# Conversion pieces of the gate weights tied to their place in VectorE's queue

## The chip, the cores and the metric

One Trainium2 chip, one core. The metric is device time in microseconds of one execution of the whole program, weights and inputs in HBM, outputs written to HBM.

## The reference

Three stages in float32, one after the other.

```python
# 1. local attention: 4 batches x 8 heads, 512 tokens + 32 global ones, head size 64
s_ll = where(|i - j| <= 32, q_l @ k_l.T / 8, -1e9);  s_lg = q_l @ k_g.T / 8
out_l = softmax([s_lg, s_ll]) @ [v_g, v_l]
out_g = softmax(q_g @ [k_g, k_l].T / 8) @ [v_g, v_l]
x = [out_g, out_l] as 2304 tokens x 512
# 2. gated layer: 512 -> 1536 -> 512
g = x @ w_gate
x = (silu(g) * (x @ w_val)) @ w_out
# 3. eight experts, 288 tokens each, given out greedily by descending logit
logits = x @ gate;  token -> expert, capacity 288
out[mask_e] = relu(x[mask_e] @ w1[e]) @ w2[e]
```

The weights of stage 2 arrive in 64-bit words, which the kernel itself turns into float32: 512 x 2 words of 32 bits per row and piece.

## The kernel before, in words

**Attention.** A unit is one batch, one half of the tokens and one pair of heads; 32 units, four of them to a half, and each has two windows `w` of 128 queries. A step is one unit and one window, in three parts that run as a pipeline over consecutive steps. `st_a` multiplies queries and keys on TensorE into the single PSUM bank S (L281), and VectorE adds the mask and takes the maximum in one instruction per head (L290), after which ScalarE makes the exponentials (L296). `st_b` transposes them (L313, banks PTa and PTb by turns) and `split_p` makes a high half on ScalarE (L304) and a low half on VectorE (L305). `st_c` multiplies with the values' high and low halves (L326, bank PV), and after the second window VectorE scales the result into `x` (L332, L333, L337). `unit_split` prepares the values: ScalarE scales and rounds (L247, L248), GpSimd takes the low half (L249). A batch's value scale (`v_scale`) needs both of its `gv` loads first; these use the same three buffers as the units. After four units `x0_t` transposes the half and splits it (L354 to L357): this is one block of 256 tokens for stage 2.

**Weights' conversion.** Stage 2's weights come in 12 slices `f` of three pieces each: gate, value and output weights. `words(f, j)` turns a piece's 64-bit words into float32 with three VectorE instructions (L173, L174, L175); each call then issues the next weight load on SyncE's queue (`load_w`, L124; three buffers). For output weights (j = 2) ScalarE makes a high half and VectorE the low one (L179, L180). For gate and value weights ScalarE sums the magnitudes (L182), TensorE adds them over the partitions (`total`, L148, into the bank that the next gate will use), `pow2` makes a power of two of the sum on VectorE (L154, L156, L157), and with it ScalarE and VectorE write the two float16 halves (L198, L199). `conv` is a generator of these pieces: five per slice, three for the first.

**Token blocks.** `first_blocks` takes three blocks of 256 tokens through the 12 slices together, since each slice's weights serve all three. Per slice and block, `gates` runs 24 matmuls (L486) into one of two G banks, ScalarE a tanh (L491), VectorE two products (L493, L495), ScalarE the high half `hh` (L497) and GpSimd the low half `hl` (L499); `out` then runs six matmuls (L509) into the block's two accumulators, one block later. The accumulators of the second and third block are the banks S, PV, PTa and PTb, so their output matmuls start only when the attention of the first four halves is done. The six other blocks follow (`moe_block`), each with the rest of the attention pulled in between; then the routing and the experts.

**Order of the work.** The program is written as generators that are stepped by turns: in the first attention one conversion step in nine attention steps (27 of these to a half, 108 in all), then one conversion step for each of the nine yields per slice of `first_blocks`. This is not the order of the queues. The tile framework schedules instructions by its own simulated clock (L1116): where an engine is free there, it takes the ready instruction that comes first in the program, so that an instruction whose inputs are ready early moves up past those that still wait. Each engine then works through its queue in the fixed order that comes out.

Of the kernel before, what the change touches and what calls it, by code (L numbers as in the profile page):

```python
# [13 lines left out]
OP = mybir.AluOpType  # L14
# [11 lines left out]
WIN = 224  # L26
UW = 1376
UK = 352
P15 = 32768.0
BIG = 3.0e38  # L30
# [3 lines left out]
def body(ctx, tc, units, gk, gv, wts, w2g, w1, w2, cst, cst2, out):  # L34
# [14 lines left out]


# [111 lines left out]
    def conv():  # L162
# [4 lines left out]
        def words(f, j):  # L167
            t = WR.pop((f, j))
            if j == 2:
                x = cv[0].tile([128, 512], I32, name="wx", bufs=2)  # L170
            else:
                x = wp_[:, f + 1, j].rearrange("p h c -> p (h c)").bitcast(I32)
            ve.tensor_scalar(x, t[:, :, 1], 3, 0x3FFFFFFF, op0=OP.logical_shift_left, op1=OP.bitwise_and)  # L173
            ve.scalar_tensor_tensor(x, t[:, :, 1], -0x40000000, x, op0=OP.bitwise_and, op1=OP.bitwise_or)  # L174
            ve.scalar_tensor_tensor(x, t[:, :, 0], 29, x, op0=OP.logical_shift_right, op1=OP.bitwise_or)  # L175
            load_w()
            x = x.bitcast(F32)
            if j == 2:
                sc.activation(oh[:, f, :], x, AF.Copy)  # L179
                ve.tensor_tensor(ol[:, f, :], x, oh[:, f, :], op=OP.subtract)  # L180
            else:
                sc.activation(junk[:, :512], x, AF.Abs, bias=tiny, accum_out=st[f][1][:, j:j + 1])  # L182
            st[f][0].append(x)

        for f in range(NF + 1):
            g = f - 1
            if g >= 0:
                xw, m = st.pop(g)
# [6 lines left out]
            if g >= 0:  # L195
                for j in range(2):
                    h, l = wp_[:, g, j, 0], wp_[:, g, j, 1]
                    sc.activation(h, xw[j], AF.Identity, scale=s[:, j:j + 1])  # L198
                    ve.scalar_tensor_tensor(l, xw[j], s[:, j:j + 1], h, op0=OP.mult, op1=OP.subtract)  # L199
# [73 lines left out]
    def st_a(u, w):  # L273
# [15 lines left out]
        for h in range(2):  # L289
            ve.tensor_tensor_reduce(sm[:, h], S[:, h, :WIN], mask[:, mv], -0.125, BIG, OP.add, OP.min,  # L290
                                    mx[:, h:h + 1])
# [8 lines left out]
    def split_p(pt, n, k):  # L300
# [4 lines left out]
        ve.scalar_tensor_tensor(pl[:q, :c], pt[:q, :c], P15, ph[:q, :c], op0=OP.mult, op1=OP.subtract)  # L305
# [146 lines left out]
    class Moe:  # L452
# [24 lines left out]
        def gates(self, f):  # L477
# [17 lines left out]
            ve.scalar_tensor_tensor(h[:, :n], t[:, :n], ib[:, 1, f:f + 1], pg[:, 1, :n], op0=OP.mult, op1=OP.mult)  # L495
# [21 lines left out]
    def first_blocks():  # L517
# [3 lines left out]
        for f in range(NF):  # L521
            while conv_done[0] < f:
                step_conv()
            for m in ms:
                yield from m.gates(f)
                yield
# [3 lines left out]
                yield  # L530
# [102 lines left out]
    for _ in first_blocks():  # L633
        step_conv()
# [51 lines left out]
    def small(shape, name, dt=F32, bufs=2):  # L686
# [5 lines left out]
    NS, SY = (mybir.DependencyInfo(c, mybir.DependencyReason.DATA)  # L692
              for c in (mybir.DependencyClass.NoSync, mybir.DependencyClass.Sync))
# [426 lines left out]
```

## Time and profile before

| | |
|---|---|
| runs, median of 3 | 987.62 us (985.96 to 990.65) |
| profiled execution: time, span | 987.89 us, 986.1 us |
| mean granted TensorE clock | 0.935 of full speed |
| TensorE busy | 876.8 us, 89% of the span |
| VectorE busy | 604.6 us, 61% |
| ScalarE busy | 473.6 us, 48% |
| GpSimd busy | 336.6 us, 34% |

The profiled execution is one of the program's runs; its span is what the trace covers, and 1.8 us of its time lie around it. Busy shares are averages over stages that differ: the first attention runs to about 160 us, the three token blocks to about 291 us, the other blocks with the rest of the attention to about 650 us, routing and experts to the end.

### The profile page before, as it was taken

The page shows a single profiled execution, that of the slowest core. Times are in us where ns is not written, and L with a number is a line of the kernel's source. Part 1 is how long each engine was busy: PE and PEld are TensorE (multiplying, and loading weights), DVE is VectorE, ACT ScalarE, POOL GpSimd, SP SyncE. Part 2 cuts the span into 40 slices and gives each one's busy share as a digit, 9 for nine tenths or more (in the row PEclk, how much of TensorE's full clock was granted, in tenths as well). Part 3 has the DMA queues.
Part 4 walks back from the last instruction along what each step waited for, and adds up shares of the span by engine and source line. Part 5 has one row for each costly group of instructions (what it writes and reads, how often), then busy time and mean ns, then how long its engine had stood idle before and what let it go on. Part 6 is the DMA issues. An engine that isn't in the chain of part 4 may idle for free.

```text
span 986.1 us, 19528 instructions
## 1 busy us (share of the span) xinstructions
PE 876.8 (89%) x7532; PEld 736.0 (75%) x7532; DVE 604.6 (61%) x1849; ACT 473.6 (48%) x1068; POOL 336.6 (34%) x324
## 2 busy tenths in 40 slices
PE   4766679999999999989989989996399899999996
PEld 3554558887788878768768757784298889889996
DVE  6998998442215749569587466265776667663210
ACT  6657676542225746457464333231344555455541
POOL 1211433431111212212211101121247867777941
PEclk9786889999999999999989999997689999999998
DMA  8766643010011321142321020000534564446610
GB/s 318 252 238 231 213 171 120 2 56 1 2 43 61 107 76 52 58 129 90 133 101 55 27 73 1 1 23 12 192 106 134 173 208 158 156 132 215 192 49 25
DMA packets 28497, 108.10 MB, mean 110 GB/s; under 512 B 3572, under 2 KB 3572, under 8 KB 28276
## 3 DMA queue, kind: packets, MB, share of 16 engines
q1 hardware_dynamic: 25332, 97.94, 29.6%
q0 software_dynamic: 3072, 8.92, 2.5%
q8 instruction: 59, 0.97, 0.4%
q14 instruction: 34, 0.28, 0.1%
HBM read 97.92 MB, written 8.91 MB: 108 GB/s over the span
## 4 chain that ended last, share of the span: by engine, by line
PE 56%; DVE 17%; DMA 13%; issue 7%; ACT 3%; POOL 3%; SPq 1%; another core or an unknown queue 0%; POOLq 0%; ACTq 0%; DVEq 0%
PE G L486 24%; PE X L509 10%; PE A L951 5%; DMA er<-w 4%; DMA wr<-wts 4%; PE A L935 3%; DMA xg<-xs,idx 2%; POOL el L882 2%; DMA unit<-gv 2%; PE rt L768 2%; DVE ptl L305 1%; DVE junk L445 1%; DVE sm L290 1%; DVE wp L175 1%; DVE kk L269 1%
## 5 line engine op out<-in xcount | busy, mean ns | idle before, releaser
L486 PEld LDWEIGHTS <-wp 128*128 128x128 f16 x2592 | 232.7, 100 | 79.2 <-issue 51.6
L486 PE MATMUL G<-xth,wp 128*128 128x256 f16 (+1 forms) x1344 | 237.9, 271 | 4.6 <-ACT xth L356 3.4
L499 POOL TENSOR_TENSOR hl<-th,hh 128x256 fp32r<-128x256 f32 (+1 forms) x108 | 80.4, 745 | 367.3 <-ACT hh L497 260.4
L486 PE MATMUL G<-xtl,wp 128*128 128x256 f16 (+1 forms) x672 | 177.8, 271 | 3.0 <-DVE xtl L357 3.0
L882 POOL TENSOR_TENSOR el<-er,eh 128x1024 fp32r<-128x1024 f32 x60 | 141.7, 2389 | 45.6 <-ACT eh L881 45.3
L493 DVE SCALAR_TENSOR_TENSOR th<-th,G 128x256 f32<-128x256 f32 (+1 forms) x108 | 43.4, 402 | 125.6 <-ACT th L491 125.4
L491 ACT ACTIVATE th<-G,ib 128x256 f32<-128x256 f32 (+1 forms) x108 | 49.5, 459 | 115.4 <-PE G L486 113.0
L881 ACT ACTIVATE eh<-er 128x1024 fp32r<-128x1024 f32 x64 | 66.7, 1056 | 58.0 <-DMA er<-w 51.5
L497 ACT ACTIVATE hh<-th 128x256 fp32r<-128x256 f32 (+1 forms) x108 | 43.5, 404 | 89.6 <-DVE th L495 89.0
L935 PE MATMUL A<-xh,eh 128*128 128x272 f32 x256 | 78.0, 305 | 0.0
L951 PE MATMUL A<-fh,eh 128*128 128x272 f32 x256 | 76.4, 301 | 0.0
L935 PE MATMUL A<-xh,el 128*128 128x272 f32 x256 | 74.9, 294 | 0.0
L935 PE MATMUL A<-xl,eh 128*128 128x272 f32 x256 | 74.9, 293 | 0.0
L951 PE MATMUL A<-fl,eh 128*128 128x272 f32 x256 | 73.8, 289 | 0.4 <-DVE fl L940 0.4
L951 PE MATMUL A<-fh,el 128*128 128x272 f32 x256 | 74.1, 291 | 0.0
L296 ACT ACTIVATE pb<-sm,mx 128x224 f32<-128x224 f32 x128 | 60.3, 472 | 24.7 <-DVE mx L290 17.2
L281 PE MATMUL S<-unit 128*128 128x224 f32 x128 | 43.9, 480 | 21.6 <-DVE mx L290 16.5
L445 DVE SCALAR_TENSOR_TENSOR junk<-xr,w2gt 128x512 f16<-128x512 f32 x80 | 58.8, 735 | 3.8 <-ACT xr L422 3.1
L509 PE MATMUL X<-oh,hh 128*128 128x512 f32 x156 | 58.0, 444 | 1.3 <-ACT hh L497 1.3
L940 DVE SCALAR_TENSOR_TENSOR fl<-A,fh 128x272 fp32r<-128x272 f32 x64 | 27.9, 439 | 50.0 <-ACT fh L939 45.4
L509 PE MATMUL X<-oh,hl 128*128 128x512 f32 x156 | 54.6, 422 | 0.0
L495 DVE SCALAR_TENSOR_TENSOR th<-th,ib,G 128x256 f32<-128x256 f32 (+1 forms) x108 | 49.9, 463 | 2.7
(288 smaller groups left out, 2141.2 us busy)
## 6 DMA issues: line engine op xcount, KB each, us to landing
er<-w SPq DMA_DIRECT2D x64, 512.0 KB, 5.6
unit<-units SPq DMA_DIRECT2D x32, 688.0 KB, 4.1
wr<-wts SPq DMA_DIRECT2D x36, 512.0 KB, 4.8
unit<-gv SPq DMA_DIRECT2D x16, 640.0 KB, 3.9
gkr<-gk SPq DMA_DIRECT2D x8, 608.0 KB, 3.4
xs<-xr SPq DMA_DIRECT2D x17, 256.0 KB, 2.0
w2gt<-w2g SPq DMA_DIRECT2D x1, 2048.0 KB
wp<-cst SPq DMA_DIRECT2D x1, 512.0 KB, 4.8
```

The costliest lines, as they stand in the source:

```text
L281: te.matmul(S[:, h, :WIN], t[:, UK + 256 * h + 128 * w:UK + 256 * h + 128 * w + 128], t[:, kw], start=True, stop=True)
L296: sc.activation(pb[:, h], sm[:, h], AF.Exp, bias=mx[:, h:h + 1], scale=-1.0, accum_out=RS[u][:, w, h:h + 1])
L445: ve.scalar_tensor_tensor(junk[:, :DM], xr, 1.0, w2gt[:, e], op0=OP.mult, op1=OP.mult, accum_out=L[:, c, e:e + 1])
L486: te.matmul(pg[:, j, :n], wp_[:, f, j, a, o], x[:, d, :n], start=(i == 0), stop=(i == 11))
L491: sc.activation(th[:, :n], pg[:, 0, :n], AF.Tanh, scale=ib[:, 0, f:f + 1])
L495: ve.scalar_tensor_tensor(h[:, :n], t[:, :n], ib[:, 1, f:f + 1], pg[:, 1, :n], op0=OP.mult, op1=OP.mult)
L499: gp.tensor_tensor(hl[:, :n], h[:, :n], hh[:, :n], op=OP.subtract)
L509: te.matmul(self.px[t], a[:, 128 * t:128 * t + 128], w[:, f, :], start=(f == 0 and i == 0), stop=(f == NF - 1 and i == 2))
L881: sc.activation(h, r, AF.Copy)
L882: q = (ve if j == 0 and i < 4 else gp).tensor_tensor(l, r, h, op=OP.subtract)
L935: behind(te.matmul(pa_[:, :CAP], a[:, s], x[:, d], start=(i == 0), stop=(i == 11)))
L951: behind(te.matmul(py[:, :CAP], a[:, s], x[:, f], start=(i == 0), stop=(i == 23)))
```

## The change

`mark` remembers the latest of certain VectorE instructions: the masked maximum (L290), the low half of the probabilities (L305) and a gate's second product (L495). `after` adds, to the first instruction of each words piece (L173) and to each gate/value low half (L199), an edge to the one remembered at that point of the program. Both are on VectorE and the edge has no semaphore: it only says that the one stands behind the other in the queue. In `first_blocks` the yields now carry the slice, and a conversion step is taken only while the conversion is less than two slices ahead; before, one was taken at every yield.

```diff
--- before.py
+++ after.py
@@ -47,6 +47,19 @@
     wk = pa.enter_context(tc.tile_pool(name="wk", bufs=2))
     ps = pa.enter_context(tc.tile_pool(name="ps", bufs=1, space=bass.MemoryType.PSUM))
 
+
+    NS, SY = (mybir.DependencyInfo(c, mybir.DependencyReason.DATA)
+              for c in (mybir.DependencyClass.NoSync, mybir.DependencyClass.Sync))
+    TURN = []
+
+    def mark(ins):
+
+        TURN[:] = [ins]
+
+    def after(ins):
+
+        if TURN:
+            tc.add_manual_dep(ins.ins, TURN[0].ins.name, NS, reason="its turn")
 
     UB = 3
     UT = {}
@@ -170,7 +183,7 @@
                 x = cv[0].tile([128, 512], I32, name="wx", bufs=2)
             else:
                 x = wp_[:, f + 1, j].rearrange("p h c -> p (h c)").bitcast(I32)
-            ve.tensor_scalar(x, t[:, :, 1], 3, 0x3FFFFFFF, op0=OP.logical_shift_left, op1=OP.bitwise_and)
+            after(ve.tensor_scalar(x, t[:, :, 1], 3, 0x3FFFFFFF, op0=OP.logical_shift_left, op1=OP.bitwise_and))
             ve.scalar_tensor_tensor(x, t[:, :, 1], -0x40000000, x, op0=OP.bitwise_and, op1=OP.bitwise_or)
             ve.scalar_tensor_tensor(x, t[:, :, 0], 29, x, op0=OP.logical_shift_right, op1=OP.bitwise_or)
             load_w()
@@ -196,7 +209,7 @@
                 for j in range(2):
                     h, l = wp_[:, g, j, 0], wp_[:, g, j, 1]
                     sc.activation(h, xw[j], AF.Identity, scale=s[:, j:j + 1])
-                    ve.scalar_tensor_tensor(l, xw[j], s[:, j:j + 1], h, op0=OP.mult, op1=OP.subtract)
+                    after(ve.scalar_tensor_tensor(l, xw[j], s[:, j:j + 1], h, op0=OP.mult, op1=OP.subtract))
                 yield g
             if f < NF:
                 words(f, 1)
@@ -287,8 +300,8 @@
         sm = wk.tile([128, 2, WIN], F32, name="sm", tag="sm")
         mx = wk.tile([128, 2], F32, name="mx")
         for h in range(2):
-            ve.tensor_tensor_reduce(sm[:, h], S[:, h, :WIN], mask[:, mv], -0.125, BIG, OP.add, OP.min,
-                                    mx[:, h:h + 1])
+            mark(ve.tensor_tensor_reduce(sm[:, h], S[:, h, :WIN], mask[:, mv], -0.125, BIG, OP.add, OP.min,
+                                         mx[:, h:h + 1]))
         if w == 0:
             RS[u] = wk.tile([128, 2, 2], F32, name="rs")
         pb = wk.tile([128, 2, WIN], F32, name="pb")
@@ -302,7 +315,7 @@
         pl = wk.tile([128, 4, 128], F16, name="ptl")
         q, c = n
         sc.activation(ph[:q, :c], pt[:q, :c], AF.Copy, scale=P15)
-        ve.scalar_tensor_tensor(pl[:q, :c], pt[:q, :c], P15, ph[:q, :c], op0=OP.mult, op1=OP.subtract)
+        mark(ve.scalar_tensor_tensor(pl[:q, :c], pt[:q, :c], P15, ph[:q, :c], op0=OP.mult, op1=OP.subtract))
         return ph, pl
 
     def st_b(u, w):
@@ -492,7 +505,8 @@
             t = th
             ve.scalar_tensor_tensor(t[:, :n], th[:, :n], 1.0, pg[:, 0, :n], op0=OP.add, op1=OP.mult)
             h = th
-            ve.scalar_tensor_tensor(h[:, :n], t[:, :n], ib[:, 1, f:f + 1], pg[:, 1, :n], op0=OP.mult, op1=OP.mult)
+            mark(ve.scalar_tensor_tensor(h[:, :n], t[:, :n], ib[:, 1, f:f + 1], pg[:, 1, :n],
+                                         op0=OP.mult, op1=OP.mult))
             hh = wk.tile([128, 256], F32R, name="hh", bufs=3)
             sc.activation(hh[:, :n], h[:, :n], AF.Copy)
             hl = wk.tile([128, 256], F32R, name="hl", bufs=3)
@@ -522,12 +536,13 @@
             while conv_done[0] < f:
                 step_conv()
             for m in ms:
-                yield from m.gates(f)
-                yield
+                for _ in m.gates(f):
+                    yield f
+                yield f
                 if last is not None:
                     last[0].out(last[1])
                 last = m, f
-                yield
+                yield f
         last[0].out(last[1])
 
     def moe_block(k):
@@ -630,8 +645,9 @@
         i += 1
         if i % 9 == 0:
             step_conv()
-    for _ in first_blocks():
-        step_conv()
+    for f in first_blocks():
+        if conv_done[0] < f + 2:
+            step_conv()
     cvs.close()
     w2p = pa.enter_context(tc.tile_pool(name="w2p", bufs=1))
     w2gt = w2p.tile([128, NE, DM], F32, name="w2gt")
@@ -689,8 +705,6 @@
     IDX, EV, ROUTED, GATHERED = {}, {}, [], []
 
     VISIT = []
-    NS, SY = (mybir.DependencyInfo(c, mybir.DependencyReason.DATA)
-              for c in (mybir.DependencyClass.NoSync, mybir.DependencyClass.Sync))
 
     def behind(ins):
 
```

## Rows read from the trace of the kernel before

**Rows 1.** Busy tenths of VectorE in 40 slices of the span (page).

```profile
DVE  6998998442215749569587466265776667663210
```

**Rows 2.** Window table: stretch, length, busy us by engine, clock, DMA share.

```profile
0.00:158.00 158.00, 107.95 (x784) 85.08 (x785) 142.83 (x387) 104.71 (x272) 38.40 (x46) 0.81 0.68 236
18.73:75.19 56.46, 40.16 (x307) 30.65 (x306) 55.53 (x149) 35.89 (x95) 11.96 (x10) 0.79 0.72 246
75.19:107.73 32.54, 22.39 (x135) 16.80 (x133) 27.44 (x78) 22.82 (x58) 8.32 (x12) 0.69 0.61 208
...
212.00:290.00 78.00, 78.00 (x577) 60.93 (x576) 17.52 (x39) 18.40 (x41) 13.79 (x19) 1.00 0.02 8
```

**Rows 3.** Timeline of VectorE, L290 of steps 3, 17, 22, 32.

```profile
18.73 0.38 DVE L290 CUSTOM_DVE_ANT_0 sm<-S,mask 128x224 f32<-128x224 f32 x1
...
75.19 0.37 DVE L290 CUSTOM_DVE_ANT_0 sm<-S,mask 128x224 f32<-128x224 f32 x1
...
107.73 0.38 DVE L290 CUSTOM_DVE_ANT_0 sm<-S,mask 128x224 f32<-128x224 f32 x1
...
157.08 0.36 DVE L290 CUSTOM_DVE_ANT_0 sm<-S,mask 128x224 f32<-128x224 f32 x1
```

**Rows 4.** Conversion by line: ns min/median/max, first and last start us.

```profile
L173 DVE TENSOR_SCALAR wp<-wr x24: 386/415/1378, 11.8 to 136.2; 128x512 int32<-128x512 int32 x24
...
L174 DVE SCALAR_TENSOR_TENSOR wp<-wr,wp x24: 655/680/694, 12.2 to 138.0; 128x512 int32<-128x512 int32 x24
...
L175 DVE SCALAR_TENSOR_TENSOR wp<-wr,wp x24: 650/681/1641, 13.2 to 141.1; 128x512 int32<-128x512 int32 x24
L175 DVE SCALAR_TENSOR_TENSOR wx<-wr,wx x12: 672/678/693, 16.7 to 148.2; 128x512 int32<-128x512 int32 x12
...
L180 DVE TENSOR_TENSOR ol<-wx,oh x12: 676/681/693, 18.1 to 151.5; 128x512 fp32r<-128x512 f32 x12
```

**Rows 5.** Groups by line, 0 to 158 us.

```profile
L281 PE MATMUL S<-unit 128*128 128x224 f32 x128 | 43.9, 480 | 21.6 <-DVE mx L290 16.5 <-DMA unit<-units 4.7
...
L326 PE MATMUL PV<-vh,pth 112*128 112x64 f16 x116 | 17.4, 210 | 9.7 <-DVE x L337 8.4 <-ACT pth L304 1.3
...
L326 PE MATMUL PV<-vh,ptl 112*128 112x64 f16 x116 | 16.0, 212 | 7.3 <-DVE ptl L305 7.3
...
L199 DVE SCALAR_TENSOR_TENSOR wp<-wp,pscw 128x512 f16<-128x512 f32 x9 | 6.6, 741 | 0.0
```

**Rows 6.** Timeline of SyncE's DMA queue, 60 to 110 us.

```profile
83.56 13.74 SPq L124 DMA_DIRECT2D wr<-wts  x6
103.18 0.33 SPq L66 DMA_DIRECT2D unit<-units  x1
```

**Rows 7.** Window table for L486 alone.

```profile
0.00:158.00 158.00, 19.85 (x138) 14.80 (x139) 0.81 0.68 236
```

**Rows 8.** Chain that ended last: start us, us, what.

```profile
214.03 2.31 PE G L486 x21
...
287.04 2.31 PE G L486 x21
```

**Rows 9.** L154 by line, and its engine's idle time before it.

```profile
L154 DVE TENSOR_SCALAR pe<-G x12: 147/159/160, 19.4 to 207.9; 128x2 int32<-128x2 int32 x12
...
  PE G L148: 9.4, 6
```

**Rows 10.** Groups by line, 160 to 298 us.

```profile
L499 POOL TENSOR_TENSOR hl<-th,hh 128x256 fp32r<-128x256 f32 x32 | 23.8, 744 | 92.6 <-ACT hh L497 31.2 <-PE PV L509 24.7 <-PE PTb L509 20.0
...
L495 DVE SCALAR_TENSOR_TENSOR th<-th,ib,G 128x256 f32<-128x256 f32 x32 | 15.3, 480 | 1.0
...
L493 DVE SCALAR_TENSOR_TENSOR th<-th,G 128x256 f32<-128x256 f32 x32 | 13.4, 421 | 68.7 <-ACT th L491 68.6
```

**Rows 11.** Timeline from 20 us, GpSimd and VectorE.

```profile
20.88 3.21 POOL L249 TENSOR_TENSOR vl<-unit,vh 112x512 f16<-112x512 f32 x2
...
21.55 1.53 DVE L175 SCALAR_TENSOR_TENSOR wp<-wr,wp 128x512 int32<-128x512 int32 x1
```

## The prediction

> **What bounds the kernel now.** I read the page's slices first, then a window table by stage, then the DVE groups and what PE waits for, and last the two places to which the work moves. VectorE is full from 20 to 160 us and then nearly empty [rows 1]. Up to 158 us it is busy for 142.8 us; ScalarE is busy for 104.7 us, TensorE for 108.0 us at a mean granted clock of 0.81 [rows 2]. At 212 to 290 us it is the other way round: PE is busy for all 78.0 us, DVE for 17.5 us [rows 2]. So the first attention is bound by DVE and the three token blocks by PE.
>
> The attention has 32 steps (unit, window); each has one pair of masked-score reductions (L290). The third step's is at 18.73 us, the 17th at 75.19, the 22nd at 107.73, the last at 157.08 [rows 3]. That is 14 steps of 4.03 us, then five in 32.5 us, where the second batch's value scale is made, then ten of 4.94 us. In the first stretch DVE is busy 55.5 of 56.5 us and ACT 35.9 us, or 2.56 us a step [rows 2].
>
> Why is DVE full? All 36 pieces of words stand in this stretch: the last third instruction of one starts at 148.2 us, the last split of the output weights at 151.5 us [rows 4]. By the program's order 12 conversion steps belong here, one in nine of 108: slices 0 and 1 and two words of slice 2, which makes 8 words, 2 output splits and 4 gate/value splits. The scheduler has hoisted the rest, because their inputs were ready.
>
> **What the change moves.** No instruction is added, none removed, and no semaphore: the new edges only order VectorE's own queue. One word costs 0.415 + 0.680 + 0.681 = 1.78 us, an output split 0.68, a gate/value split 0.74 [rows 4, 5]. Out of the stretch go 28 words (49.7 us), 10 output splits (6.8) and 5 of the 9 gate/value splits (3.7): **60.2 us of DVE**. This is queue time, and not the gain.
>
> *The gain in the attention.* PE is idle for 16.5 us before score matmuls until DVE's maxima, 8.4 us before the value matmuls until DVE has taken the previous unit's result (L337), and 7.3 us until DVE's low halves (L305): **32.2 us** [rows 5]. The bounds: none returns, if a chain through ACT is as late; or the stage shrinks to ACT's 104.7 us, which is 53 us. A second route gives about the same: halfway between 4.03 us and ACT's 2.56 saves 0.74 us a step, 18 us over 24 steps. In the turn, six weight loads in SP's queue held it from 83.56 us for 13.7 us, and the next unit's load went out at 103.18 [rows 6]; with the loads following the pieces some 13 us of this go. That is 31 us. I take 32.2, the measured waits. A step that waits less for DVE will wait next for ACT's exponentials.
>
> *What moves with it.* Every word issues the next weight load on SP. 28 loads less 3 prefetched ones leave the stretch, so that unit and value loads stand behind fewer of them; in the token blocks three per 12 us meet a DMA that is 2% busy [rows 2]. Their wait is for DVE's release of the buffer, and the load of the routing weights, queued behind the last of them on SP, is needed only after the fourth block: nothing. The pieces' ACT work (abs, high halves) goes too, into a stage where ACT is busy for 18.4 of 78 us [rows 2]: nothing, while that cover lasts.
>
> *Gates that fitted into the old stretch.* 138 gate matmuls, 5.75 gates of 24, ran before 158 us [rows 7]. With slice 1's split now the 11th of the 12 steps and less idle PE, I give four. From 214.03 to 287.04 us 18 gates pass, 4.06 us each, of which 2.6 are gate matmuls (2.31 us for 21 of 24) [rows 8]. So 1.75 x 2.6 = **4.6 us** is lost; bounds 0 (all still fit) and 15 (none does).
>
> *The token blocks.* One slice (three gates) lasts 12.17 us on PE. DVE's conversion needs 3 x 1.78 + 0.68 + 2 x 0.74 + three small ones of 0.16 [rows 4, 5, 9] = 8.0 us per slice, the gates 3 x (0.48 + 0.42) = 2.7 us [rows 10]: 10.7 of 12.17 us. It fits, but the pieces come in the first five of nine steps, so two gates meet nearly all of it. The trace has no slice with all of this. Bounds: 0, and 4 us (the slower rival). I take 0.4 us, near the lower end, as the conversion runs two slices ahead of its use and DVE's need lies below PE's: **4 us** over ten slices.
>
> [...] GpSimd's low halves of the values ran from 20.88 us, two in 3.21 us, and inside them a third word instruction took 1.53 us against its median of 0.68 [rows 4, 11]. In the token blocks GpSimd makes one hl of 0.74 us per gate [rows 10]. [...]
>
> *Sum.* 987.9 (profiled execution; span 986.1 and 1.8 around it) - 32.2 + 4.6 + 4 = 964.3. The median of the runs is 987.6, 0.3 less: **964**. The later stages have no conversion in them and shift as they are.
>
> **The rivals.**
> 1. *The stage falls to ACT's time*: 53 us instead of 32.2, 944. For it: DVE also slows ACT, whose queue is idle a third of the time. Against: each step is a chain over PE, DVE, ACT, PE, ACT, DVE with one bank for scores. Chance 0.15.
> 2. *VectorE becomes the bound of the token blocks through GpSimd*: each of three hl holds it for its 0.74 us, 10.7 + 2.2 = 12.9 us against 12.17; some 0.75 us x 10 slices in place of the 4, so 968; with the in-order waits for the scale's matmul (9.4 us in six [rows 9], 1.6 a slice) 14.5, which makes 23 us and 983. For it: rows 11. Against: an hl takes 0.74 of a gate's 4.06 us, and only what DVE starts inside it is held. Chance 0.11.
> 3. *Another wait takes the place of DVE's*: half of the 32.2 stays, as PE at a clock of 0.7 in the turn [rows 2] and ACT's chain are nearly as late: 980. Chance 0.12.
> 4. *It doesn't do what it says*: only the first instruction of a piece is pinned, to a place no earlier than its mark, and the scheduler fills the gaps as tightly: 988. Against: the pin alone forbids the hoist. Chance 0.05.
> 5. *Slower: the bank of the scale.* The matmul that sums a slice's magnitudes takes the bank of the next gate; that gate starts only when DVE has read the sum. Before, the words were done long ahead. Now the second word stands behind the last gate's L495, then 1.78 us and an ACT pass, and if the third word and its split (2.5 us) go ahead of the read on DVE, PE stands for up to 4 us per slice. At 4 x 10 = 40 us it gives 987.9 - 32.2 + 4.6 + 40 = 1000; from 2.8 us per slice on, the gain is gone. For it: DVE waited for that matmul six times [rows 9]. Against: the scheduler sees the wait and orders PE's queue by it. Chance 0.09.
>
> **How the numbers follow.** The forecast (955 to 974) has 0.48. A measurement of this kernel tells about 0.5%, 5 us, from no change. Faster by more: 0.48 + 0.15 + 0.11 and some 0.07 of rival 3 = 0.81; within: 0.05 of rival 3 and rival 4, 0.10; slower 0.09. The range runs from 940, just under rival 1, to 985, which takes in rivals 2 and 3 and leaves out 5 and most of 4.
>
> **What would show it.** Right: in the window up to the last L290, about 32 us earlier than 157, DVE has slack; some 8 words start there, the others among the L495s; the idle of L281, L326 before DVE shrinks below half of 32 us; slices keep 12.2 to 12.6 us. Wrong: words still crowd the attention (4), DVE slack with unchanged pitch (3), PE idle before L486 behind L148 or L154 (5), third word instructions above 1 us beside POOL (2).

## The result, and the profile after

| | before | after |
|---|---|---|
| runs, median of 4 | 987.21 us | 971.30 us |
| lowest to highest | 985.96 to 990.65 | 969.81 to 974.83 |
| profiled execution: time, span | 987.89, 986.1 us | 974.83, 973.1 us |
| mean granted TensorE clock | 0.935 | 0.954 |

The ratio is 0.9839, with a 95% interval of 0.9802 to 0.9875: 1.6% faster. The forecast was 964, the range 940 to 985; the gain is 15.9 us where 23.6 were forecast. The profiled execution after is the slowest of its four, so its own gain is 13.1 us.

In the changed kernel lines of the helpers stand 13 or 14 lower: the masked maximum is L303 (was L290), the score matmul L294 (L281), the value matmul L339 (L326), the words L186 to L188 (L173 to L175), the sum over partitions L161 (L148), its ACT pass L195 (L182), the gate matmul L499 (L486), a gate's second product L508 (L495), GpSimd's low half L513 (L499), the output matmul L523 (L509).

In the profile's rows PE is TensorE, PEld its weight load, DVE VectorE, ACT ScalarE, POOL GpSimd and SP SyncE.

First the page, three rows of its 40 slices of the kernel after. Of these the DVE row answers to [rows 1].

```profile
PE   5777699999999999989989989995498899999996
DVE  3877968888227578489496484266775677674210
PEclk9979899999999999999979999998599999999998
```

VectorE is no longer full from the second to the seventh slice and nearly empty behind them: its work goes on to the tenth. The last pair of masked maxima now starts at 110.91 us instead of 157.08 [rows 3], 46 us earlier. Eight words start before 112 us, the number that was forecast:

```profile
L187 DVE SCALAR_TENSOR_TENSOR wp<-wr,wp x6: 676/692/1530, 22.6 to 102.5; 128x512 int32<-128x512 int32 x6
L187 DVE SCALAR_TENSOR_TENSOR wx<-wr,wx x2: 679/684/689, 39.9 to 81.3; 128x512 int32<-128x512 int32 x2
```

They are not quite the eight that were meant. The second word of slice 2 is tied to the attention's last low half (L318, 114.03 us) and starts at 114.63 us; in its place stands the first word of slice 3, whose edge names the first gate's second product, and that one is at 77.44 us.

The steps of [rows 3] show where the attention became shorter. The third, 17th, 22nd and last pair of maxima are now at 19.04, 55.27, 75.12 and 110.91 us. The three stretches between them, after:

```profile
19.04:55.27 36.23, 28.10 (x275) 22.59 (x272) 30.57 (x104) 30.60 (x90) 9.85 (x9) 1.00 0.55 183
55.27:75.12 19.85, 14.67 (x108) 12.04 (x106) 12.86 (x49) 15.48 (x41) 2.88 (x7) 0.74 0.42 153
75.12:110.91 35.79, 25.35 (x261) 20.46 (x259) 29.43 (x86) 28.79 (x79) 11.69 (x10) 0.95 0.58 184
```

The first 14 steps lost 20.2 us (2.59 us a step instead of 4.03), the turn to the second batch 12.7, the last ten steps 13.6. In the turn both VectorE's pieces and the weight loads in front of the unit loads became fewer; no run separates the two.

Yet only 13 of these 46 us reach the end of the profiled execution. Where they go is best read from one window table: up to the last maxima, from there to the 36th gate of the three token blocks (its second product starts at 290.08 us before and at 275.39 after), and both together. The columns are those of [rows 2]: length, busy time of PE, PEld, DVE, ACT and POOL with the number of instructions, granted clock, DMA's busy share, GB/s. TensorE's idle time is the length less its busy time. The kernel before:

```profile
0.00:157.50 157.50, 107.45 (x780) 84.61 (x781) 142.38 (x385) 104.21 (x271) 37.90 (x44) 0.80 0.68 235
157.50:290.00 132.50, 132.44 (x1000) 105.25 (x999) 47.74 (x115) 51.34 (x118) 35.23 (x62) 1.00 0.06 23
0.00:290.00 290.00, 239.89 (x1777) 189.86 (x1778) 190.12 (x499) 155.55 (x388) 73.13 (x105) 0.89 0.40 138
```

The kernel after:

```profile
0.00:111.50 111.50, 77.14 (x674) 61.68 (x674) 79.49 (x270) 85.59 (x234) 25.87 (x31) 0.94 0.59 199
111.50:275.30 163.80, 152.75 (x1106) 120.13 (x1105) 114.80 (x230) 69.59 (x156) 53.41 (x74) 0.97 0.31 109
0.00:275.30 275.30, 229.89 (x1777) 181.81 (x1778) 194.29 (x499) 155.18 (x388) 79.28 (x105) 0.96 0.42 146
```

The last row of each holds the same 1777 TensorE instructions, so the two can be set against each other as a ledger. Idle time of TensorE in the attention fell from 50.05 to 34.36 us (−15.7). Behind the attention it rose from 0.06 to 11.05 us (+11.0). The 1777 instructions themselves took 10.0 us less, at a mean granted clock of 0.96 instead of 0.89. Together −15.7 + 11.0 − 10.0 = **−14.7 us**, the 36th gate's gain. The rest of the 46 us was never a gain: token-block matmuls that had run in the old attention left it. Of gate matmuls alone 19.40 us stood before 157.5 us, and 3.38 us before 111.5 us after.

That the 10.0 us are the clock's can be seen by matching TensorE's instructions with the granted clock in the two traces, where it stands at one of two levels, 1.00 and 0.50 of full speed (after, 1.00 from 111.5 to 116.3 us and 0.50 from 116.3 to 123.1). A score matmul takes 353 ns (median) at the upper level and 581 at the lower in both kernels, a gate matmul 272 and 421. Before, TensorE was busy for 48.4 us at the lower level on the way to the 36th gate, after for 19.2 us. At these durations 29 us less at the lower level save a third and more, 10 to 11 us: an estimate that agrees with the measured 10.0.

From there on nothing changes by more than 1.2 us. The last gate matmul starts 379.5 us behind the 36th gate before (669.6, so the other blocks end some 20 us behind the 650 given above) and 380.1 us after (655.4); from it to the end of the span it is 316.5 and 317.6 us.

What TensorE waited for in the attention, by line, after (0 to 111.5 us; answers to [rows 5]):

```profile
L294 PE MATMUL S<-unit 128*128 128x224 f32 x128 | 36.9, 417 | 13.6 <-DVE mx L303 8.2 <-DMA unit<-units 5.3
L339 PE MATMUL PV<-vh,pth 112*128 112x64 f16 x120 | 16.0, 197 | 2.9 <-DVE x L350 1.7 <-ACT pth L317 0.8 <-ACT vh L261 0.3
L339 PE MATMUL PV<-vh,ptl 112*128 112x64 f16 x120 | 14.4, 199 | 5.0 <-DVE ptl L318 4.9
```

The three waits for DVE were 16.5, 8.4 and 7.3 us; now they are 8.2, 1.7 and 4.9: 14.8 of 32.2 us remain. Laid over VectorE's own instructions in the traces, these waits show why. Before, VectorE was at work on a conversion piece for 18.1 of the 32.2 us; after, for 3.6 of the 14.8. What is left is in the main the instruction itself that TensorE waits for: 12.2 us of the 16.5 before score matmuls were the maxima's own time, and 7.1 of the 8.2 still are. VectorE is idle for only 0.3 us in the remaining waits.

The same 128 score matmuls take 417 ns instead of 480 in the mean, the value matmuls 197 to 199 instead of 209 to 212: fewer of them ran at the lower clock (of the 128 score matmuls 25 took over 500 ns, and 58 before).

What TensorE waits for behind the attention was nothing before. After, from 111.5 to 275.3 us (waited for: us in total, times, longest):

```profile
PE G L499 <- DVE th L508: 6.9, 10, 2.0
PE PTb L367 <- DVE x L350: 1.9, 1, 1.9
PE PV L339 <- DVE ptl L318: 0.7, 1, 0.7
PE G L161 <- ACT junk L195: 0.6, 4, 0.2
PE PV L339 <- DVE x L350: 0.4, 1, 0.4
```

Two places. At the **seam**, 111.5 to 128 us, TensorE is idle for 4.4 us at a clock of 0.79 (the lower level from 116.3 to 123.1 us). The last unit's scaling (L350) stands behind five instructions of slice 2's words on DVE; their edges name the last low half, and the scaling is not marked:

```profile
114.03 0.68 DVE L318 SCALAR_TENSOR_TENSOR ptl<-PTa,pth 112x512 f16<-112x512 f32 x1
114.63 0.42 DVE L186 TENSOR_SCALAR wp<-wr 128x512 int32<-128x512 int32 x1
114.97 0.42 DVE L186 TENSOR_SCALAR wx<-wr 128x512 int32<-128x512 int32 x1
...
117.11 0.42 DVE L350 TENSOR_TENSOR x<-PV,rs 128x256 f32<-128x256 f32 x1
```

And the first gate matmuls of the third block take 0.42 us each, against 0.27 us later on. In the **slices**, 128 to 275.3 us, it is idle for 6.6 us, nearly all of it before a gate whose G bank DVE has not yet read (L508). Seven slices, from one second product to the same one seven slices later, on DVE's timeline:

```profile
142.67 0.48 DVE L508 SCALAR_TENSOR_TENSOR th<-th,ib,G 128x256 f32<-128x256 f32 x1
...
235.56 0.48 DVE L508 SCALAR_TENSOR_TENSOR th<-th,ib,G 128x256 f32<-128x256 f32 x1
```

92.89 / 7 = 13.27 us a slice, where [rows 8] gave 12.17. In that stretch TensorE is busy for 88.83 us: 12.69 busy and 0.58 idle a slice. Of the 0.52 us that it is busier, 0.38 are the two matmuls of the sum (L161), which the slices of [rows 8] no longer had. Of the idle time 0.43 us a slice is the wait for a G bank and up to 0.16 the wait for the sum's magnitudes. The second product that holds the bank is not behind a piece: VectorE stands idle before it until the tanh is done. One of the seven slices, the others have the same pair of rows:

```profile
166.05 0.42 DVE L506 SCALAR_TENSOR_TENSOR th<-th,G 128x256 f32<-128x256 f32 x1 [1.44 <-ACT th L504]
166.51 0.48 DVE L508 SCALAR_TENSOR_TENSOR th<-th,ib,G 128x256 f32<-128x256 f32 x1
```

What differs is the order on TensorE. The three gates of a slice, 4.06 us apart in the kernel before, now follow one another after 2.7, 3.1 and 7.5 us, so that one gate needs a bank again before the chain of tanh and two products has emptied it.

### The profile page after: what moved, and what is told of

The parts are those of the page before. It is cut to its first block, busy times and chain, and to the rows that moved or that the text cites. A ratio compares the mean times of both kernels' runs of the same rounds, so it can differ in the third digit from the quotient of the medians.

```text
span 973.1 us, 19541 instructions
## 1 busy us (share of the span) xinstructions
PE 865.8 (89%) x7532; PEld 727.4 (75%) x7532; DVE 608.5 (63%) x1849; ACT 472.9 (49%) x1068; POOL 341.6 (35%) x324
## 5 line engine op out<-in xcount | busy, mean ns | idle before, releaser
L499 PEld LDWEIGHTS <-wp 128*128 128x128 f16 x2592 | 235.1, 100 | 85.1 <-issue 57.1
L499 PE MATMUL G<-xth,wp 128*128 128x256 f16 (+1 forms) x1344 | 235.1, 271 | 11.9 <-DVE th L508 8.4
L513 POOL TENSOR_TENSOR hl<-th,hh 128x256 fp32r<-128x256 f32 (+1 forms) x108 | 82.1, 760 | 365.3 <-ACT hh L511 310.7
L499 PE MATMUL G<-xtl,wp 128*128 128x256 f16 (+1 forms) x672 | 177.8, 270 | 3.0 <-DVE xtl L370 3.0
L954 DVE SCALAR_TENSOR_TENSOR fl<-A,fh 128x272 fp32r<-128x272 f32 x64 | 27.9, 439 | 53.7 <-ACT fh L953 52.9
L523 PE MATMUL X<-oh,hh 128*128 128x512 f32 x156 | 57.7, 442 | 1.3 <-ACT hh L511 1.3
L523 PE MATMUL X<-oh,hl 128*128 128x512 f32 x156 | 54.8, 422 | 0.0
L303 DVE CUSTOM_DVE_ANT_0 sm<-S,mask 128x224 f32<-128x224 f32 x128 | 44.6, 384 | 15.0 <-PE S L294 7.2
L508 DVE SCALAR_TENSOR_TENSOR th<-th,ib,G 128x256 f32<-128x256 f32 (+1 forms) x108 | 50.0, 463 | 2.9
```

The source lines that it names most:

```text
L303: mark(ve.tensor_tensor_reduce(sm[:, h], S[:, h, :WIN], mask[:, mv], -0.125, BIG, OP.add, OP.min, mx[:, h:h + 1]))
L499: te.matmul(pg[:, j, :n], wp_[:, f, j, a, o], x[:, d, :n], start=(i == 0), stop=(i == 11))
L508: mark(ve.scalar_tensor_tensor(h[:, :n], t[:, :n], ib[:, 1, f:f + 1], pg[:, 1, :n], op0=OP.mult, op1=OP.mult))
L513: gp.tensor_tensor(hl[:, :n], h[:, :n], hh[:, :n], op=OP.subtract)
L523: te.matmul(self.px[t], a[:, 128 * t:128 * t + 128], w[:, f, :], start=(f == 0 and i == 0), stop=(f == NF - 1 and i == 2))
```

## The experiments

Each was run against the kernel before on the same chip; kernels of different rounds are compared through their ratios, and most of all through the traces. The table gives, for each profiled execution, the start of the last pair of maxima, TensorE's idle time up to the 36th gate, the mean clock up to there, the 36th gate's second product, the last gate matmul, and the ratio with its 95% interval.

| kernel | last max | idle | clock | 36th gate | last gate MM | median us | ratio |
|---|---|---|---|---|---|---|---|
| before | 157 | 50.1 | 0.89 | 290.1 | 669.6 | | 1 |
| after | 111 | 45.4 | 0.96 | 275.4 | 655.4 | 971.3 | 0.9839 [0.9802, 0.9875] |
| nopins | 157 | 51.2 | 0.89 | 291.4 | 671.2 | 986.7 | 0.9978 [0.9954, 1.0002] |
| oldpace | 110 | 70.1 | 0.92 | 312.9 | 691.7 | 1011.5 | 1.0239 [1.0210, 1.0269] |
| attpins | 107 | 57.6 | 0.93 | 291.8 | 671.2 | 988.4 | 0.9995 [0.9968, 1.0022] |
| blockpins | 126 | 44.2 | 0.96 | 271.2 | 656.2 | 975.1 | 0.9875 [0.9838, 0.9912] |
| late | 113 | 42.0 | 0.96 | 273.6 | 659.3 | 974.0 | 0.9836 [0.9801, 0.9871] |
| late1 | 113 | 39.6 | 0.97 | 266.6 | 653.0 | 966.8 | 0.9785 [0.9733, 0.9837] |
| spread | 107 | 38.0 | 0.97 | 264.2 | 644.4 | 962.0 | 0.9750 [0.9695, 0.9804] |
| pow | 110 | 39.2 | 0.94 | 269.9 | 650.0 | 966.1 | 0.9781 [0.9729, 0.9832] |
| seven | 117 | 46.4 | 0.95 | 276.7 | 657.3 | 971.5 | 0.9842 [0.9788, 0.9897] |
| latespread | 113 | 44.9 | 0.98 | 271.1 | 655.5 | 974.2 | 0.9848 [0.9824, 0.9873] |
| spreadpow | 110 | 35.7 | 0.96 | 263.6 | 643.6 | 963.8 | 0.9744 [0.9719, 0.9768] |
| seam | 111 | 42.2 | 0.96 | 271.8 | 656.9 | 975.1 | 0.9878 [0.9835, 0.9920] |

The routing and experts behind the last gate matmul took 311 to 321 us in these profiles, with no edit in them, so a few us between two medians prove nothing; the columns before that are the better reading.

**The two halves of the change, one at a time.** `nopins` keeps the new pace of `first_blocks` and drops the edges:

```diff
-        if TURN:
+        if False:
```

> Changed kernel without the edges in VectorE's queue; the pace of at most two slices ahead stays. If the edges make the gain: all words crowd into the attention again, last masked maximum near 155 us, 984 to 990 us. Rival (the pace makes the gain, since work placed later in the program has a lower rank): last masked maximum near 120 us, 968 to 976 us.

The last maximum is at 157 us, and the run can't be told from the kernel before. The pace alone does nothing that can be measured: without an edge the pieces are hoisted into the attention as before. This is what was expected of the edges.

`oldpace` keeps the edges and takes a conversion step at every yield again:

```diff
-        if conv_done[0] < f + 2:
-            step_conv()
+        step_conv()
```

> Changed kernel with the edges, but with a conversion step at every one of the nine yields per slice, as before the change. If the pace matters: the conversion is done by slice 6, VectorE needs some 17 us per slice of 12 us there and bounds those slices, 975 to 985 us. If only the edges matter: 968 to 974 us, the attention the same as in the changed kernel.

The attention is as short as in the changed kernel, and the program is 23 us slower than before. TensorE's waits, 127 to 250 us of this kernel:

```profile
PE G L161 <- ACT junk L195: 10.5, 6, 3.0
PE X L523 <- ACT hh L511: 5.9, 3, 2.7
PE PTa L523 <- ACT hh L511: 5.8, 3, 2.7
PE S L523 <- ACT hh L511: 5.6, 3, 2.7
```

TensorE waits up to 3.0 us for the ACT pass over the second word before it may sum the slice's magnitudes; the gates that queue behind that sum are late, and then the outputs wait for their `hh`. From the third gate (127.34 us) to the 18th (238.48) a slice takes 22 us. The expectation had VectorE's load as the bound, 17 us a slice and 975 to 985 us. The load is no more than a part of it: from 108 to 250 us VectorE is busy for 96.3 of 142 us, and the waits in the order of the queues come on top. This is the prediction's fifth rival, at the pace that the change also gave up. So the four corners are: neither half 988, pace alone 987, edges alone 1011, both 971.

**Which of the marks matter.** `attpins` leaves the two marks of the attention and drops the one on a gate's second product:

```diff
-            mark(ve.scalar_tensor_tensor(h[:, :n], t[:, :n], ib[:, 1, f:f + 1], pg[:, 1, :n],
-                                         op0=OP.mult, op1=OP.mult))
+            ve.scalar_tensor_tensor(h[:, :n], t[:, :n], ib[:, 1, f:f + 1], pg[:, 1, :n],
+                                    op0=OP.mult, op1=OP.mult)
```

> Changed kernel, but the gates' second product is no longer a place to stand behind: pieces of the token blocks are tied to the end of the attention only and may be hoisted up to there. If the ties inside the token blocks cost (the sum of the magnitudes comes late, 13.27 us per slice instead of 12.17): words move up, the sums are early, slices fall to about 12.5 us, 964 to 969 us. Rival (the ties there protect the gates' own VectorE work): the words crowd in after the attention, the first gates are late, 974 to 982 us.

The attention is as short as any, and the whole gain is given back. The rival's mechanism is the right one, but at 988 us it costs more than its 974 to 982. The window table of this kernel behind its attention (columns as above):

```profile
100.00:120.00 20.00, 11.45 (x131) 8.81 (x130) 19.52 (x50) 14.37 (x39) 5.26 (x4) 0.87 0.33 113
120.00:140.00 20.00, 13.13 (x79) 9.92 (x78) 17.17 (x33) 6.86 (x15) 3.83 (x6) 0.78 0.62 205
140.00:160.00 20.00, 13.64 (x78) 10.04 (x78) 17.25 (x35) 6.95 (x14) 8.38 (x7) 0.74 0.54 188
160.00:180.00 20.00, 15.51 (x108) 12.18 (x106) 17.30 (x36) 8.13 (x18) 5.84 (x7) 1.00 0.55 190
```

The 28 words that are left, tied only to the end of the attention, crowd right behind it: DVE is busy for 71.2 of 80 us, TensorE for 53.7. A gate's products stand among them on DVE (behind two gates at 130.6 us the next ones are at 143.4 and 155.2), and gate matmuls of this kernel wait 17.5 us for the bank, in six waits. The full VectorE has moved from one stage to the next.

`blockpins` does the reverse, with no mark in the attention:

```diff
-            mark(ve.tensor_tensor_reduce(sm[:, h], S[:, h, :WIN], mask[:, mv], -0.125, BIG, OP.add, OP.min,
-                                         mx[:, h:h + 1]))
+            ve.tensor_tensor_reduce(sm[:, h], S[:, h, :WIN], mask[:, mv], -0.125, BIG, OP.add, OP.min,
+                                    mx[:, h:h + 1])
...
-        mark(ve.scalar_tensor_tensor(pl[:q, :c], pt[:q, :c], P15, ph[:q, :c], op0=OP.mult, op1=OP.subtract))
+        ve.scalar_tensor_tensor(pl[:q, :c], pt[:q, :c], P15, ph[:q, :c], op0=OP.mult, op1=OP.subtract)
```

> Changed kernel with the ties behind gates only: the attention's own two marks are left out, so that the 12 steps of the attention are free, while all later pieces still stand behind a gate's second product. If it is the hoisting out of the token blocks that fills VectorE: last masked maximum at 108 to 116 us and 966 to 974 us, as in the changed kernel. Rival (the pieces must also be held back within the attention): last masked maximum at 125 us or later, 977 us or more.

The attention is some 15 us longer than in the changed kernel, its 36th gate is 4 us earlier, and the total can't be told from that of the changed kernel. Neither half of the expectation holds as written: the last maximum is where the rival put it, the total near where the theory did. So the mark on a gate's second product, which spreads the pieces over the slices, makes most of the gain (without it there is none, with it alone 1.2% of the 1.6); how long the attention lasts says little.

**The seam.** `late` takes no step at the first eight yields of `first_blocks`, so that the first slice's gates are free of conversion work:

```diff
-    for f in first_blocks():
-        if conv_done[0] < f + 2:
+    for n, f in enumerate(first_blocks()):
+        if n >= 8 and conv_done[0] < f + 2:
```

> Changed kernel, but the first conversion step of the token blocks is traced after the third gate of slice 0, so that the sum of slice 2's magnitudes no longer stands before the second and third gate. Theory (the bank of the scale at the seam): these two gates run inside the attention again, three gates before the last masked maximum where the changed kernel has one, and the last gate of the three blocks comes some 8 to 12 us earlier; 959 to 964 us. Rival (TensorE and VectorE have no room for gates in the shorter attention): the gates run there, but the last masked maximum moves later by about as much; 969 to 973 us.

Three gates now run inside the attention, as the theory had it, and the total can't be told from the changed kernel's (959 to 964 us had been expected). The next gates are at 117.3 and 131.2 us, the slices stay at 13.27 us, the 36th gate is only 1.8 us earlier, and the blocks behind it take 385.7 us instead of 380.1.

`late1` lets the conversion run one slice less ahead on top of that:

```diff
+        if n >= 8 and conv_done[0] < f + 1:
```

> As the late start (first conversion step after slice 0's third gate), but the conversion is then kept one slice ahead, not two, so that slice 1 hasn't nine steps to catch up. Theory (in the late start the three gates won at the seam were lost again by the nine steps crowded into slice 1): gates come at an even pace from the fourth on, the last gate near 266 to 270 us, 963 to 967 us. Rival (VectorE at the seam is what delays the first gates, whatever their banks): no earlier than in the late start, 971 to 976 us.

The 36th gate (266.6 us) comes 7 us before that of `late`, within the expectation, as does the total. But the gates are not at the even pace that was to bring it (117.2, 131.1, 132.0 us), and the slices are not shorter (13.39 us): the sixth, seventh and eighth gate are at 132.0, 137.1 and 144.3 us instead of 135.6, 140.0 and 150.8.

`seven` takes a conversion step in seven attention steps instead of nine, so that more stands in the attention:

```diff
-        if i % 9 == 0:
+        if i % 7 == 0:
```

> Changed kernel with a conversion step at every seventh attention step, not every ninth: 15 steps in the attention, among them the rest of slice 2's words and its sum, which then stands ahead of slice 0's gates. Theory (the seam costs since that sum is late and holds the second gate): last masked maximum 2 to 5 us later than 111, but the token blocks start right behind it, with one slice less to convert there; last gate near 268 us, 962 to 967 us. Rival (VectorE has no slack in the attention's second half): last masked maximum at 118 us or later, 970 to 975 us.

The attention is 6 us longer, the slices are the same, and so is the total: the theory's gain doesn't come.

**The slices.** `spread` takes a step at every second yield of a slice (five of nine), where the change takes them at the first five:

```diff
+    for n, f in enumerate(first_blocks()):
+        if n % 9 % 2 == 0 and conv_done[0] < f + 2:
```

> Changed kernel with the five conversion steps of a slice at every second of its nine yields, not at the first five. If crowding in the first two gates makes the 13.27 us per slice: 12.4 to 12.8 us per slice, 964 to 968 us. Rival (the sum's matmul waits for ScalarE's magnitudes wherever the pieces stand, since the piece before it is tied to the gate before): 13.3 us per slice, 969 to 974 us.

This is the best by its median (`spreadpow` is by its ratio). Its interval against the kernel before lies well below 1. The changed kernel ran in another round: its four runs, 969.8 to 974.8 us, all lie above the 959.9 to 964.6 us of these four, and its 36th gate is 11 us later. Two slices take 25.11 us (152.72 to 177.83, 202.94, 228.05), 12.55 each, the 36th gate is at 264.2 us. The window from 153 to 235 us, first of the changed kernel:

```profile
153.00:235.00 82.00, 78.10 (x570) 61.72 (x570) 68.36 (x130) 36.41 (x80) 31.43 (x43) 1.00 0.34 112
```

Then of `spread`, with the whole stretch to its 36th gate above it:

```profile
0.00:264.10 264.10, 226.15 (x1777) 180.57 (x1778) 194.57 (x499) 155.15 (x388) 70.21 (x105) 0.97 0.44 152
153.00:235.00 82.00, 81.94 (x603) 64.73 (x602) 73.69 (x139) 39.38 (x90) 26.98 (x44) 1.00 0.35 116
```

TensorE stands still for 0.06 us of 82 instead of 3.9: the same pieces, in other places of the same queue, cost TensorE nothing but the sum's own matmuls (12.17 + 0.38 = 12.55). Its gates come 4.2 to 4.5 us apart, but for one of six (3.0). Why the place of VectorE's pieces changes the order of TensorE's gates is not shown: the framework's simulated clock decides it. The row to the 36th gate is 226.15 us busy and 38.0 idle, against 229.9 and 45.4.

`pow` changes the place of the sum instead: the first word's step goes ahead of the sum and the power of two.

```diff
-            if g >= 0:
-                xw, m = st.pop(g)
-                s = pow2(total(m, 2), 2, iw[:, :, g])
-                yield
             if f < NF:
...
                 words(f, 0)
                 yield
+            if g >= 0:
+                xw, m = st.pop(g)
+                s = pow2(total(m, 2), 2, iw[:, :, g])
+                yield
```

> Changed kernel with the sum of a slice's magnitudes one piece later (after the next slice's first word instead of before it). Theory (per slice, TensorE waits 0.57 us for the magnitudes before the sum's weights and 0.43 us for a bank): the first wait vanishes, 12.6 to 12.8 us per slice, 964 to 968 us. Rival (the wait moves to the bank of the next gate): 13.2 us or more per slice, 970 to 975 us.

Its slices are 12.51 us, with no wait for the sum, though the steps still stand in the first five yields. Its first gates are later (two from 130.1 us on and one at 135.4, where the changed kernel has 127.1 and 132.4 and `spread` 125.3, 127.8 and 132.0), and its 36th is at 269.9 us, behind that of `spread`. Two different edits that take the waits for the sum and the bank away give the same slice, so these waits are most of what the 13.27 us have over it.

`spreadpow` has both edits:

> The spread steps together with the sum one piece later. If the sum's wait for the magnitudes is still part of the spread kernel's 12.5 us: 12.3 us per slice, 957 to 961 us. Rival (with spread steps the sum finds its magnitudes ready; 12.17 us of matmuls and 0.25 us of the sum itself are what is left): 12.4 to 12.6 us per slice, 960 to 967 us.

12.65 us a slice, 36th gate at 263.6 us: no more than `spread` alone, as the rival had it.

`latespread` joins `late` and `spread`:

```diff
+        if n >= 8 and n % 9 % 2 == 0 and conv_done[0] < f + 2:
```

> Both repairs together: first conversion step after slice 0's third gate, and five steps per slice at every second yield, two slices ahead at most. If the seam and the slices are separate losses: three gates before the last masked maximum, 12.5 us per slice, last gate near 258 to 262 us, 954 to 960 us. Rival (the steps left out of slice 0 are missing later, so that some slice has to wait for its weights): 960 to 967 us, with idle time of TensorE before a gate of slice 2 or 3.

The early start undoes the good slice: 13.96 us, and the wait for a G bank is back. So is the one that the rival named, for a slice's weights (L212 is their low half). This kernel, 153 to 235 us:

```profile
PE G L499 <- DVE th L508: 5.1, 5, 1.0
PE G L499 <- DVE wp L212: 1.7, 6, 0.3
```

`seam` (the last one) keeps `spread` from slice 1 on and in slice 0 takes one step at the first yield and three at the last, so that slice 2's sum does not sit in the third block's bank:

```diff
+    for n, f in enumerate(first_blocks()):
+        if n < 9:
+            for _ in range({0: 1, 8: 3}.get(n, 0)):
+                step_conv()
+        elif n % 9 % 2 == 0 and conv_done[0] < f + 2:
+            step_conv()
```

> The spread kernel with slice 0's pieces moved round its gates: the first step (a word) at the first yield, the next three (with the sum that takes a gate's bank) together behind the third gate; from slice 1 on the same steps at the same yields as in the spread kernel. Theory (at the seam the sum's bank holds back two gates): three gates before the last masked maximum instead of one, slices of 12.5 us, last gate near 255 to 259 us where the spread kernel has it at 264, 954 to 958 us if the later stages keep their length. Rival (what is won at the seam is lost again behind it, as in the late start): last gate at 261 us or later, 960 to 966 us.

The theory falls. A gate stands at 131.2 us and none in the 25 us before it; in `late`, `late1` and `latespread` one stands at 130.7 to 131.2 us too, with a single one (117.2 to 117.4) in between. And the slices are 13.74 us with the same wait for a bank as in `latespread`:

```profile
PE G L499 <- DVE th L508: 6.1, 6, 1.0
```

Of the four kernels with three early gates only `late1` is clearly better than the changed kernel, and none is better than `spread`. What holds a gate at 131 us in all four, and why the slices of `latespread` and `seam` are long again, stays open. So does a third thing: in these four and in `blockpins` it is 384 to 386 us from the 36th gate to the last gate matmul, in all the others 379 to 381.

## Why the prediction was right, and where it was off

**That it gains, and by about how much: right, with some luck in the sum.** Conversion pieces on DVE did hold up the old attention, the edges did keep them out (eight words, as counted), and the price behind stayed smaller than the gain. The sum was −32.2 + 4.6 + 4 = −23.6 us; the ledger reads −15.7 (idle, attention) + 4.4 (idle, seam) + 6.6 (idle, slices) − 10.0 (busy time, by the clock) = −14.7. Without the last term, which the prediction doesn't have, it would be −4.7. Of the signs that were named, the words and the waits for DVE (below half of 32 us) came; the attention is 46 us shorter and not 32, and a slice takes 13.27 us and not 12.2 to 12.6.

**The step that was mis-sized is "the gain in the attention: I take 32.2, the measured waits".** 14.8 of these 32.2 us are still there. A wait that the profile puts down to DVE also holds the time of the very instruction that is waited for, and no edge takes that away: conversion pieces filled only 18.1 of the 32.2 us. The three waits fell by 17.4 us and idle time by 15.7. The third rival had half of the 32.2 stay and priced it at 980. It was right on the size, but its reason (the clock in the turn, ACT's chain) is not what the waits show, and it missed the total through the same missing term: the granted clock in the attention went from 0.80 to 0.94, and the matmuls were shorter (a score matmul 417 ns in the mean instead of 480).

"A second route" was right in one part: the turn lost 12.7 us where it had 13. The other part, 18 us for the shorter steps, was 34. That both routes gave about 32 us is chance, and neither number reaches the 36th gate. The first rival, ACT's time for the whole stage, did not come, though it came near in the first 14 steps: 2.59 us each against the 2.56 that ACT had been busy, with ACT now busy for 30.6 of 36.2 us, and VectorE as long. Over the stage ACT is busy for 85.6 of 111.5 us.

**"Gates that fitted into the old stretch", 4.6 us, was the wrong account.** More gates left than forecast: one (24 matmuls) stands ahead of the last maxima, not four. But a gate that leaves takes its matmuls with it, and the attention becomes shorter by as much. What costs is only idle time that appears where the work lands. At the seam this was 4.4 us, near the 4.6 by chance, and in the rows it is the words ahead of the last scaling (1.9), the low half and `x` before value matmuls (1.1), and a G bank (1.5).

**"The token blocks", 4 us by ten slices, was low.** The idle time there is 6.6 us; with the sum's matmuls a slice is 1.10 us longer, not 0.4. The reason given was that DVE's need (10.7 us) lies below TensorE's. It does, and in `spread` the slice is 12.55 us, 0.38 over [rows 8], almost as forecast. What the step left out is that the pieces in the first five of nine steps go with another order of TensorE's queue: gates that follow each other closely wait for a bank (0.43 us a slice), and the sum waits a little for its magnitudes. The fifth rival had the wait for the sum, at up to 4 us a slice. In the changed kernel it is small. `oldpace` shows it at full size: 1011, 23 us over the kernel before, even more than the 1000 that the rival gave. The prediction has no term for the pace of `first_blocks`, which is what holds this down.

**The second rival, VectorE held up beside GpSimd, is seen and does not decide.** The timeline of the changed kernel, VectorE and GpSimd at 170 us:

```profile
170.06 0.69 DVE L187 SCALAR_TENSOR_TENSOR wp<-wr,wp 128x512 int32<-128x512 int32 x1
170.22 1.13 POOL L513 TENSOR_TENSOR hl<-th,hh 128x256 fp32r<-128x256 f32 x1 [1.93 <-ACT hh L511]
...
170.79 1.11 DVE L188 SCALAR_TENSOR_TENSOR wp<-wr,wp 128x512 int32<-128x512 int32 x1
```

`hl` starts inside one word instruction and the next one starts inside `hl`; both take 1.1 us, where `hl` took 0.74 in the mean of [rows 10] and the word instruction 0.68 in the median of [rows 4]. The whole traces show the same of VectorE. Of the 72 second and third word instructions seven took over 0.70 us before (1.02 to 1.64) and 20 after (1.10 to 1.53), and all of these began inside an instruction of GpSimd; those that began outside one, 60 before and 44 after, took 0.65 to 0.70. Not all that begin inside are longer: five of 12 before and eight of 28 after are not. That each `hl` holds VectorE for its 0.74 us, 2.2 us a slice, was the rival's estimate. In the seven slices from 142.67 us on three instructions a slice are longer, L187, L188 and L212: 1.15, 1.11 and 1.27 us where 0.68, 0.68 and 0.74 are usual, 1.4 us together. In `spread` GpSimd's `hl` is even longer in the mean, over the same 153 to 235 us:

```profile
L513 POOL TENSOR_TENSOR hl<-th,hh 128x256 fp32r<-128x256 f32 x20 | 18.6, 932 | 46.9 <-ACT hh L511 46.9
```

In the changed kernel that mean is 854 ns. Yet the slices of `spread` are the shorter ones and TensorE does not wait in them. In the changed kernel one of the longer words (L188) stands before the ACT pass for the sum, so it can explain TensorE's 0.16 us there; the wait for a G bank, 0.43 us, comes behind products that start after VectorE has stood idle. No run has these slices without GpSimd's instructions.

**The fourth rival** (it doesn't do what it says, since the scheduler fills the gaps as tightly) is out: with the edges the pieces left the attention, and in `nopins`, without them, they did not.

## What to carry to other kernels

Before you call the shorter stage a gain, make a ledger over a stretch that holds the same instructions in both kernels: busy and idle time of the engine that bounds the end. Here the attention ended 46 us earlier and 14.7 us were left, and `attpins`, with a still shorter attention, had none. Before you call a wait for an engine a gain, look at what that engine does in it: only what the change takes away can be won, and not the instruction that is waited for. Where work is moved beside another engine's in-order queue, where its pieces stand there can count for more than whether they fit: by the pace alone the same pieces made the program 1.6% faster, 2.5% faster, or 2.4% slower. And a stage whose busy engine runs below its full clock may give back more, or in another way, than its waits show: here 10.0 of the 14.7 us were TensorE's busy time, at a mean clock of 0.96 instead of 0.89.

## What was not expected of the hardware

How much of the gain came by the granted clock: 0.80 in the old attention, where TensorE was idle for 50.05 of 157.5 us, 0.94 in the new one with 34.36 of 111.5, and with it shorter matmuls, so that 10.0 of the 14.7 us to the 36th gate are busy time. At the new seam it was 0.79 again: TensorE had been busy for 3.1 of the 4.8 us before it fell at 116.3 us, and for 5.5 of the 6.8 us before it rose at 123.1. The share of idle time does not order the stretches by clock: TensorE was idle for 32% of the old attention (0.80) and 31% of the new one (0.94), and inside the new one for 26% of the turn (0.74) and 29% of the ten steps behind it (0.95). What sets the clock is not shown: no run tried it by itself, and `pow`, with 39.2 us of idle time to the 36th gate at a mean of 0.94, doesn't fit a simple order either.
